# RWKV-7 attention with a merged mixture on one Trainium2 core: the state turned by whole transposes, and TensorE held to the order of the program text

## The chip, the cores and the metric

The kernel runs on one core of a Trainium2 chip. All data is in fp32. The metric is the device time of one execution in microseconds.

A core has five engines that run their own instruction queues and wait for one another by semaphores. TensorE does matrix products (the profile's PE, with its weight loads as PEld) and writes PSUM. VectorE (DVE), ScalarE (ACT) and GpSimd (POOL) do the elementwise work. SyncE (SP) issues most of the DMAs.

## What is computed

A recurrent attention block (4 batches, 8 heads, 768 tokens, head size 40) feeds a mixture of four experts (model width 320, hidden width 1024).

```python
def _attn_ref(r, k, v, w, a, b):
    for t in range(S):
        y[:, :, t] = np.einsum('bhd,bhde->bhe', rt, state)
        Sa = np.einsum('bhde,bhe->bhd', state, at)
        state_decay = state * wt[:, :, None, :] - np.einsum('bhd,bhe->bhde', Sa, bt)
        state = state_decay + np.einsum('bhd,bhe->bhde', vt, kt)

def _moe_ref(x, domain_probs, w1, w2):
    p = domain_probs / (domain_probs.sum(-1, keepdims=True) + 1e-09)
    for e in range(E):
        h = np.maximum(x @ w1[e], 0.0)
        out += p[:, e:e + 1] * (h @ w2[e])
```

## The kernel before

**Units.** The 768 tokens are cut into 12 chunks of 64, and the 4 batches into 2 pairs. One chunk of one pair is a unit: 24 units, numbered so that unit u is chunk u // 2 of pair u % 2. Inside a unit the recurrence is written as products of 64x64 blocks; from chunk to chunk only a state per batch and head is carried (`state`, one tile per batch, heads in four pairs j of two heads s). Unit u therefore needs the state that unit u - 2 has left.

**Stages of a unit.** `within` prepares what doesn't need the state: decays (`G`), transposes of the decay (`pg`) and of the scaled keys (`n_tok` to `NT` through `pNT`, `k_tok` to `KT` through `pKT`), score blocks (`pc`, `pf` in `F`, `pe` in `ET`, `pev` in `EV`). `substitute` inverts a triangular block of `F`: `blocks` are copied by VectorE and ScalarE, turned into `M` by VectorE, and a row-by-row elimination writes `Z`, from unit 2 on in some 60 small instructions of GpSimd (L559, L572). `merge` turns `Z` into `Qc` and `QTc` (VectorE, L583 and L585; both are kept in the order of the program text) and completes the inverse with the products `pY` and `pQ`. `step` brings in the state: `RH` (products of the state with `AT`), `psat` (copied to `SaT` and `SX`), `pxr` (two terms, one masked into `SX`, the other copied to `RS`), and `pdy`, from which VectorE makes the output `Y` and the new state. `Y` is brought to the layout of the mixture by products with `pick` (`pxT`, first two chunks) or by DMAs, as `xT`.

**The mixture.** Two units of a chunk go through the experts together. Its pieces wait in a list (`todo`): `up_last` and `up_main` (tile `ph`, lines 738 and 752, relu to `hs`), and `products` (tile `p`, line 873), seven half-size products in place of eight, with sums of weights and of `hs` made by VectorE (`a`). Each unit takes pieces from the list at four gaps. Units 0 and 1 use a plain form (`po`).

**The order.** The loop over u at the end calls the generators `w` (`within` of unit u + 2), `w_next`, `m` (`merge` of u + 1), `s` and `s_next` (`step` of u and u + 1), and the gaps in a written order; u < 5 is "early" and has an order of its own. A scheduler then places the instructions on each engine by its own estimates of when their inputs are ready. Only those wrapped in `tc.keep_in_program_order` keep the order of the text among themselves. On TensorE this concerns few before the change; on VectorE `Qc`, `QTc` and the first instructions of `substitute`, but not `Y`, the state updates, `n_tok` or `k_tok`.

**Quadrants.** Products of 64x64 blocks use a quarter of TensorE's array. `quadrants` issues them in an order in which four following ones use the four quarters: `row` is the half of the input partitions, `col` that of the output partitions. PSUM has five banks for tiles of tag `big` and three for `mm`, each in turn. In `step` the transposed state `SN`, needed by `pxr`'s second term, is made by 16 such products with an identity (`psn`, in the same two banks as `prh`; the profile shows both as `prn`).

Of the kernel before, what the change touches and what calls it, by code (L numbers as in the profile page):

```python
# [7 lines left out]
FP32 = mybir.dt.float32  # L8
# [7 lines left out]
def kernel(  # L16
# [53 lines left out]
    ps = ctx.enter_context(tc.tile_pool(name="ps", bufs=1, space=bass.MemoryType.PSUM))  # L70

# [121 lines left out]
    def load_raw(q, names):  # L193
# [3 lines left out]
        for x in names:  # L197
# [3 lines left out]
            for r in range(2):  # L201
                if x in "RV":

                    sets = ((slice(0, 8, 2), slice(r, 16, 4)), (slice(1, 8, 2), slice(3 - r, 16, 4)))
                else:
                    sets = ((slice(0, 8), slice(r, 16, 2)),)
# [99 lines left out]
    def normalize():  # L306
# [3 lines left out]
        for e in range(E):  # L310
            nc.tensor.transpose(out=pp[:, e * n:(e + 1) * n], in_=flat[:, :, e], identity=ident[0:n, 0:n])
# [24 lines left out]
    def turn(name, src, pinned=False):  # L336

        p = big(name)
        for j in range(NJ):
            ins = nc.tensor.transpose(out=p[:, j * P:(j + 1) * P], in_=src(j), identity=ident[:])  # L340
            if pinned and j == 0:
                tc.keep_in_program_order(ins)
# [14 lines left out]
    def d_half(j, s):  # L357
        return s ^ (j % 2)

    def of_d_half(x, r):  # L360

        return x.rearrange("p (jj four) e -> p jj four e", four=4)[:, :, slice(1, 3) if r else slice(0, 4, 3), :]

    BY_TOKENS = [(j, s, i) for j in range(NJ) for s, i in QUADS]
    BY_PAIRS = [(2 * j + x, s, i) for i in range(2) for j in range(2) for s, x in QUADS]
# [4 lines left out]
    def quadrants(p, lo, order, out_cols, *terms):  # L370


        for j, s, i in order:
            for n, term in enumerate(terms):
                row, col, at, lhsT, rhs = term(j, s, i)
                nc.tensor.matmul(  # L376
# [12 lines left out]
    def within(q):  # L389
# [31 lines left out]
        def turn_rv():  # L421
            VT = sb.tile([P, 2 * NJ, L], FP32, name="VT", tag="turned", bufs=3)
            q.RT = sb.tile([P, 2 * NJ, L], FP32, name="RT", tag="RT", bufs=2)
            for x, t in (("V", VT), ("R", q.RT)):
# [4 lines left out]
                to = t[:].rearrange("p (i j) t -> p j i t", i=2)  # L429
                nc.scalar.copy(out=to[:, 0::2], in_=p[:, 0::2])  # L430
                for r in range(2):
                    nc.scalar.copy(out=to[half(r), 1::2], in_=p[half(1 - r), 1::2])
# [145 lines left out]
    def merge(q):  # L578
# [16 lines left out]
        def two_heads(name, lhsT, rhs, to):  # L595
            p = big(name)
            for n in range(NJ):
                for r in range(2):
                    nc.tensor.matmul(  # L599
# [14 lines left out]

    def step(q, xT):
# [27 lines left out]
        psa = quadrants(p, 0, BY_TOKENS, L, lambda j, s, i: (  # L643
            i ^ s, d_half(j, s), j, RH[half(i ^ s), head(j, s), :], q.QT[half(i ^ s), head(j, s), :],
# [521 lines left out]
```

## Time and profile before

| | |
|---|---|
| Median of three runs | 1132.29 us (1129.44 to 1134.07) |
| The profiled execution | 1129.6 us |
| Its span, first to last instruction | 1127.5 us |
| Mean granted TensorE clock | 0.986 |
| TensorE busy in the whole span | 1083.1 us |
| TensorE's 16 `psn` products, one step (573.86 to 574.36) | 0.50 us |
| `pNT`'s four transposes (571.94 to 572.38) | 0.44 us |
| Chain that ended last: share of PE, of POOL | 67%, 10% |

A record of the profile gives an engine's instruction with its line, its operation, the tile that it writes, those that it reads, and its form. Several of one kind in a row are merged into one line with their number. Each quadrant product has two records. The time in square brackets is the engine's idle time before the instruction, with what ended it. Durations on TensorE overlap, so the time of a group there is read from its start to the start of the next.

### The profile page before, as it was taken

What the parts mean: (1) busy time and instruction counts of PE and PEld (TensorE: products, weight loads), DVE (VectorE), ACT (ScalarE), POOL (GpSimd) and SP (SyncE); (2) the same over time, 40 slices, a digit from 0 to 9 for tenths busy, and PEclk for the clock granted to TensorE, in tenths of its full rate; (3) what the DMA queues carried; (4) which work ended last, traced back from release to release, by engine and by line L of the source; (5) the groups of instructions that cost most, each with busy time, mean ns of one, the idle gap of its engine ahead of it and who ended that gap; (6) DMA issues with size and microseconds to landing.
All of it is one profiled execution on the core that took longest, in us unless ns stands there. A gap on an engine that the chain in (4) does not pass through costs nothing.

```text
span 1127.5 us, 38551 instructions
## 1 busy us (share of the span) xinstructions
PE 1083.1 (96%) x16100; PEld 963.2 (85%) x16100; DVE 758.8 (67%) x1553; ACT 353.0 (31%) x956; POOL 498.8 (44%) x1272
## 2 busy tenths in 40 slices
PE   6899997999999999999999999999999999999998
PEld 5777776788989889988989989989899999888887
DVE  8766547797766767677677677677677686553343
ACT  2323423332332332432432332332333323321110
POOL 5005727754625526437437347346346356340000
PEclk7899998999999999999999999999999999999999
DMA  7784553245253543644543543544553442231320
GB/s 118 214 239 125 130 113 71 71 108 126 77 130 88 122 102 99 141 103 93 143 104 88 143 103 90 142 96 96 133 114 86 122 110 63 76 90 57 108 90 12
DMA packets 268868, 122.18 MB, mean 108 GB/s; under 512 B 213736, under 2 KB 242072, under 8 KB 268696
## 3 DMA queue, kind: packets, MB, share of 16 engines
q1 hardware_dynamic: 265416, 119.12, 43.4%
q8 instruction: 127, 2.08, 0.8%
q10 hardware_dynamic: 3280, 0.61, 0.3%
q14 instruction: 45, 0.37, 0.1%
HBM read 111.79 MB, written 3.93 MB: 103 GB/s over the span
## 4 chain that ended last, share of the span: by engine, by line
PE 67%; POOL 10%; DVE 7%; issue 4%; ACT 2%; SPq 1%; DMA 1%; DVEq 0%; POOLq 0%
PE p L873 23%; PE ph L752 22%; PE ph L738 7%; POOL Z L572 6%; POOL Z L559 4%; PE pdy L376 2%; PE psat L376 2%; PE po L796 2%; DVE M L534 1%; PE pxr L376 1%; PE prn L376 1%; PE pQ L599 1%; PE pfe L376 1%; DVE G L406 1%; PE pc L376 1%
## 5 line engine op out<-in xcount | busy, mean ns | idle before, releaser
L752 PE MATMUL ph<-xT,w1p 128*128 128x256 f32 (+1 forms) x1520 | 342.7, 378 | 1.7 <-issue 1.7
L752 PEld LDWEIGHTS ph<-xT,w1p 128*128 128x128 f32 x1520 | 273.4, 190 | 63.1 <-issue 25.6
L572 POOL TENSOR_TENSOR Z<-Z 128x31 f32<-128x31 f32 (+7 forms) x704 | 257.2, 365 | 55.2
L867 DVE TENSOR_TENSOR a<-hs 128x512 f32<-128x512 f32 x220 | 153.8, 716 | 104.6 <-ACT hs L757 104.6
L559 POOL TENSOR_TENSOR Z<-M,Z 128x62 f32<-128x62 f32 (+7 forms) x352 | 144.0, 409 | 134.5 <-DVE M L550 108.7
L757 ACT ACTIVATE hs<-ph 128x512 f32<-128x512 f32 (+1 forms) x208 | 115.3, 564 | 235.3 <-PE ph L752 234.3
L873 PE MATMUL p<-sums,a 128*128 128x160 f32 x1056 | 165.1, 299 | 0.0
L873 PEld LDWEIGHTS p<-sums,a 128*128 128x128 f32 x1056 | 152.9, 190 | 2.3
L773 DVE SCALAR_TENSOR_TENSOR osb<-p,gate,osb 128x320 f32<-128x320 f32 (+1 forms) x243 | 107.9, 482 | 55.3 <-PE p L873 52.1
L531 POOL COPY below<-F 32x256 f32<-32x256 f32 x48 | 23.4, 488 | 219.5 <-ACT F L489 217.8
L738 PE MATMUL ph<-xT,w1p 64*64 64x256 f32 (+1 forms) x1520 | 111.1, 379 | 5.4 <-issue 5.4
L873 PE MATMUL p<-w,a 128*128 128x160 f32 x704 | 105.8, 301 | 0.9 <-ACT hs L757 0.5
L873 PE MATMUL p<-w,hs 128*128 128x160 f32 x704 | 102.9, 299 | 0.0
L873 PEld LDWEIGHTS p<-w,hs 128*128 128x128 f32 x704 | 100.3, 190 | 2.2
L873 PEld LDWEIGHTS p<-w,a 128*128 128x128 f32 x704 | 98.3, 190 | 3.6 <-ACT hs L757 3.6
L591 POOL COPY QT<-QTc 32x256 f32<-32x256 f32 x96 | 49.3, 513 | 91.4 <-DVE QTc L585 44.9
L738 PEld LDWEIGHTS ph<-xT,w1p 64*64 64x64 f32 x1520 | 66.1, 135 | 14.3 <-issue 9.8
L534 DVE STREAM_TRANSPOSE M<-blocks 128x1024 f32<-128x1024 f32 x24 | 47.2, 1968 | 33.9 <-ACT blocks L528 33.7
L679 ACT COPY RS<-pxr 64x256 f32<-64x256 f32 x88 | 32.2, 366 | 115.0 <-DVE SX L387 73.6
L419 DVE RECIPROCAL gp<-gp 128x320 f32<-128x320 f32 x24 | 51.7, 2153 | 0.8
L516 ACT COPY EV<-pev 64x160 f32<-64x160 f32 x96 | 23.4, 286 | 88.1 <-PE pev L376 87.7
L583 DVE STREAM_TRANSPOSE Qc<-Z 128x256 f32<-128x256 f32 x24 | 15.1, 631 | 49.1 <-POOL Z L572 48.9
(151 smaller groups left out, 1427.9 us busy)
## 6 DMA issues: line engine op xcount, KB each, us to landing
w1p<-in_moe_w_dram SPq DMA_DIRECT2D x95, 512.0 KB
w1p<-in_moe_w_dram SPq DMA_DIRECT2D x190, 64.0 KB
w<-in_moe_w_dram SPq DMA_DIRECT2D x4, 1280.0 KB
sums<-in_moe_w_dram SPq DMA_DIRECT2D x9, 512.0 KB
natW<-in_w_dram SPq DMA_DIRECT2D x48, 80.0 KB
natB<-in_b_dram SPq DMA_DIRECT2D x48, 80.0 KB
natK<-in_k_dram SPq DMA_DIRECT2D x48, 80.0 KB
out_dram<-osb SPq DMA_DIRECT2D x46, 80.0 KB
```

Of the source, the lines that this page charges most:

```text
L376: nc.tensor.matmul(out=p[row][half(col), lo + at * out_cols:lo + (at + 1) * out_cols], lhsT=lhsT, rhs=rhs, start=(n == 0), stop=(n == len( ...
L419: pin(nc.vector.reciprocal(out=gp[:], in_=gp[:]))
L534: ins = nc.vector.transpose(out=M[:], in_=cols)
L559: ins = eng.tensor_tensor(out=Z[:, 1:3, 0:n, j + 1:Q], in0=M[:, j:j + 2, None, j + 1:Q].to_broadcast([P, 2, n, m]), in1=Z[:, here, 0:n, j: ...
L572: eng.tensor_tensor(out=z[:, 0], in0=z[:, 0], in1=z[:, x], op=ALU.add)
L591: ins = nc.gpsimd.tensor_copy(out=q.QT[quarter(i), :, quarter(i % 2)], in_=QTc[quarter(i)])
L738: nc.tensor.matmul(out=ph[i][half(c), f, :], lhsT=w1.last[part(i), f, half(c)], rhs=xT[part(i), 2, :], start=(f == 0), stop=False,)
L752: nc.tensor.matmul(out=ph[i][:, f, :], lhsT=w1.main[:, g, at * P:(at + 1) * P], rhs=xT[:, g, :], start=False, stop=(g == 1 and f == HF // ...
L757: nc.scalar.activation(out=h[:, i * HF // 2:(i + 1) * HF // 2, 0:n], in_=ph[i][:], func=ACTF.Relu,)
L773: nc.vector.scalar_tensor_tensor(out=to, in0=p, scalar=sc, in1=to, op0=ALU.mult, op1=ALU.add)
L867: nc.vector.tensor_tensor(out=t[:], in0=x, in1=y, op=op)
L873: nc.tensor.matmul(out=p[:, n * HD:(n + 1) * HD], lhsT=a[:, f, :], rhs=b[:, f, :], start=(f == 0), stop=(f == HF - 1),)
```

## The change

Four things are done.

- `matmul` and `transpose` wrap every TensorE instruction in `keep_in_program_order`.
- The 16 `psn` products of `step` go. A new function `turn_state` makes four full 128x128 transposes of the state into a bank of their own and one copy to `SN`, which has its own buffer. The loop calls it for unit u + 1 after the decay's transposes (`pg`) of unit u + 2. Tiles of tag `step` get two buffers in place of three.
- Which head lies in which half of `VT`, `RT`, `SaT`, `SX` and `RS` is set by j % 2 in place of s ^ (j % 2). The orders of the quadrants, the DMAs of the raw inputs and the copies of `VT` and `RT` (four of 64 partitions each, where there were one of 128 and two of 64) and of `RS` (two in place of four) follow from this.
- In the loop for u >= 5, `merge`'s first product and the first part of the next `step` (`prh`) come before `pc`, and `merge`'s second product comes after the first part of an up piece (`lead`), before its main part.

The order in which TensorE's instructions stand in the compiled kernels, one unit of the steady part, by tile and number of products:

```
before: pNT 4  pKT 4  pc 16  prn 32  pY 8  ph 16  p 16  pQ 8  pfe 16  ph 8  psat 32  ph 8  p 12  pe 16  pxr 32  ph 16  p 16  pg 4  pev 16  pdy 32  ph 16  p 12
after:  pNT 4  pKT 4  pY 8  prh 16  pc 16  ph 8  pQ 8  ph 8  p 16  pfe 16  ph 8  psat 32  ph 8  p 12  pe 16  pxr 32  ph 16  p 16  pg 4  psn 4  pev 16  pdy 32  ph 16  p 12
```

and VectorE's, around the merge of unit 14:

```
before: RT  Y 2  state  Y  state 2  n_tok  state  k_tok  Qc  G  QTc  G
after:  RT  Qc  Y 2  state  Y  state 2  n_tok  state  k_tok  QTc  G 2
```

The diff, without the places where only the name of the call changes:

```diff
@@ -69,6 +69,12 @@
     sb = ctx.enter_context(tc.tile_pool(name="sb", bufs=1))
     ps = ctx.enter_context(tc.tile_pool(name="ps", bufs=1, space=bass.MemoryType.PSUM))
 
+    def matmul(**k):
+        return tc.keep_in_program_order(nc.tensor.matmul(**k))
+
+    def transpose(**k):
+        return tc.keep_in_program_order(nc.tensor.transpose(**k))
+
     def big(name):
         return ps.tile([P, 512], FP32, name=name, tag="big", bufs=5)
 
@@ -201,7 +207,7 @@
             for r in range(2):
                 if x in "RV":
 
-                    sets = ((slice(0, 8, 2), slice(r, 16, 4)), (slice(1, 8, 2), slice(3 - r, 16, 4)))
+                    sets = [(slice(y, 8, 2), slice(2 * r + y, 16, 4)) for y in range(2)]
                 else:
                     sets = ((slice(0, 8), slice(r, 16, 2)),)
                 for n, hs in sets:
...
@@ -354,15 +360,17 @@
     def head(j, s):
         return 2 * j + s
 
-    def d_half(j, s):
-        return s ^ (j % 2)
+    def of_d(x, j, s, i, n=64):
+        return x[64 * (j % 2):64 * (j % 2) + n, 4 * i + 2 * (j // 2) + s, :]
 
     def of_d_half(x, r):
 
-        return x.rearrange("p (jj four) e -> p jj four e", four=4)[:, :, slice(1, 3) if r else slice(0, 4, 3), :]
+        return x.rearrange("p (jj four) e -> p jj four e", four=4)[:, :, 2 * r:2 * r + 2, :]
 
     BY_TOKENS = [(j, s, i) for j in range(NJ) for s, i in QUADS]
-    BY_PAIRS = [(2 * j + x, s, i) for i in range(2) for j in range(2) for s, x in QUADS]
+    BY_D_TOKENS = [(2 * jj + r, s, i) for jj in range(2) for s in range(2) for r, i in QUADS]
+    BY_TOKENS_D = [(2 * jj + x, s, r ^ s) for jj in range(2) for s in range(2) for r, x in QUADS]
+    BY_D_HEADS = [(2 * jj + r, s, i) for jj in range(2) for i in range(2) for r, s in QUADS]
 
     def banks(name):
         return [big(f"{name}{x}") for x in range(2)]
...
@@ -426,10 +434,10 @@
                     turn_raw(t[:], n["raw" + x][:])
                     continue
                 p = turn(f"p{x}T", tok(n["padded" + x]), q.u == 1)[:].rearrange("p (j i t) -> p j i t", i=2, t=L)
-                to = t[:].rearrange("p (i j) t -> p j i t", i=2)
-                nc.scalar.copy(out=to[:, 0::2], in_=p[:, 0::2])
+                to = t[:].rearrange("p (i jj s) t -> p s jj i t", i=2, s=2)
                 for r in range(2):
-                    nc.scalar.copy(out=to[half(r), 1::2], in_=p[half(1 - r), 1::2])
+                    for y in range(2):
+                        nc.scalar.copy(out=to[half(r), y], in_=p[half(y), r::2])
             return VT
 
         if q.u == 1:
@@ -445,8 +453,8 @@
             return n["paddedV"][:, :, 0:D] if q.u < PADDED else n["V"][:]
 
         def causal_scores(VT):
-            pc = quadrants(banks("pc"), 0, BY_TOKENS, L, lambda j, s, i: (
-                d_half(j, s), i, j, of_slots(VT, d_half(j, s), j, i, D), of_slots(q.RT, d_half(j, s), j, i, D),
+            pc = quadrants(banks("pc"), 0, BY_D_TOKENS, L, lambda j, s, i: (
+                j % 2, i, 2 * (j // 2) + s, of_d(VT, j, s, i, D), of_d(q.RT, j, s, i, D),
             ))
             for r in range(2):
                 pin(causal(of_d_half(q.VC[:, :, D:D + L], r), pc[r]), q.start)
...
@@ -612,6 +620,19 @@
         two_heads("pQ", Qc, Y, q.QT[:, :, quarter(1)])
         yield
 
+    def turn_state(q):
+
+        if q.start:
+            return
+        psn = big("psn")
+        for i in range(2):
+            for jj in range(2):
+                x = state[q.b[i]][:, 2 * jj:2 * jj + 2, :].rearrange("p j d -> p (j d)")
+                at = (2 * i + jj) * P
+                transpose(out=psn[:, at:at + P], in_=x, identity=ident[:])
+        q.SN = sb.tile([P, 2, 2, 2, 64], FP32, name="SN", tag="SN", bufs=1)
+        nc.scalar.copy(out=q.SN[:].rearrange("p i jj s e -> p (i jj s e)"), in_=psn[:])
+
     def step(q, xT):
 
         st = [state[bb] for bb in q.b]
@@ -620,28 +641,20 @@
         if q.start:
             RH = q.EV
         else:
-            p = banks("prn")
-            prh = quadrants(p, 0, BY_TOKENS, D, lambda j, s, i: (
+            prh = quadrants(banks("prh"), 0, BY_TOKENS, D, lambda j, s, i: (
                 s, i ^ s, j, of_slots(q.AT, s, j, i), st[i][half(s), j, 0:D],
-            ))
-
-            psn = quadrants(p, NJ * D, BY_PAIRS, 64, lambda j, s, i: (
-                s, d_half(j, s), 2 * i + j // 2, st[i][half(s), j, :], ident[half(s), half(s)],
             ))
             RH = RHs()
             for s in range(2):
                 nc.vector.tensor_tensor(
                     out=of_slot(RH[:], s)[:, :, 0:D], in0=prh[s], in1=of_slot(q.EV[:], s)[:, :, 0:D], op=ALU.add,
                 )
-            SN = sb.tile([P, 2, 2 * 2, 64], FP32, name="SN", tag="step", bufs=3)
-            for s in range(2):
-                nc.scalar.copy(out=SN[:, s], in_=psn[s])
         yield
 
 
         p = banks("psat")
-        psa = quadrants(p, 0, BY_TOKENS, L, lambda j, s, i: (
-            i ^ s, d_half(j, s), j, RH[half(i ^ s), head(j, s), :], q.QT[half(i ^ s), head(j, s), :],
+        psa = quadrants(p, 0, BY_TOKENS_D, L, lambda j, s, i: (
+            i ^ s, j % 2, 2 * (j // 2) + s, RH[half(i ^ s), head(j, s), :], q.QT[half(i ^ s), head(j, s), :],
         ))
         SX = SXs()
         if not q.end:
@@ -649,7 +662,7 @@
             pst = quadrants(*at, BY_TOKENS, D, lambda j, s, i: (
                 i ^ s, i, j, q.QT[half(i ^ s), head(j, s), :], RH[half(i ^ s), head(j, s), 0:D],
             ))
-        SaT = sb.tile([P, NJ, 2, L], FP32, name="SaT", tag="step", bufs=3)
+        SaT = sb.tile([P, NJ, 2, L], FP32, name="SaT", tag="step", bufs=2)
         for x in range(2):
             nc.scalar.copy(out=SaT[:, :, x, :], in_=psa[x])
         if not q.end:
@@ -660,25 +673,21 @@
         yield
 
         p = banks("pxr")
-        px = quadrants(p, 0, BY_TOKENS, L, lambda j, s, i: (
-            d_half(j, s), i, j, SaT[half(d_half(j, s)), j, i ^ s, :], of_slots(q.RT, d_half(j, s), j, i),
+        px = quadrants(p, 0, BY_D_TOKENS, L, lambda j, s, i: (
+            j % 2, i, 2 * (j // 2) + s, SaT[half(j % 2), 2 * (j // 2) + s, i ^ s, :], of_d(q.RT, j, s, i),
         ))
         if not q.start:
-            prs = quadrants(p, NJ * L, BY_PAIRS, L, lambda j, s, i: (
-                d_half(j, s), s, 2 * (j // 2) + i, SN[half(d_half(j, s)), s, 2 * i + j // 2, :],
-                of_slots(q.RT, d_half(j, s), j, i),
+            prs = quadrants(p, NJ * L, BY_D_HEADS, L, lambda j, s, i: (
+                j % 2, s, 2 * (j // 2) + i, q.SN[half(j % 2), i, j // 2, s, :], of_d(q.RT, j, s, i),
             ))
         for x in range(2):
             ins = causal(of_d_half(SX[:, :, D:D + L], x), px[x])
             if q.u == 0:
                 tc.keep_in_program_order(ins)
         if not q.start:
-            RS = sb.tile([P, NJ, 2, L], FP32, name="RS", tag="step", bufs=3)
+            RS = sb.tile([P, NJ, 2, L], FP32, name="RS", tag="step", bufs=2)
             for x in range(2):
-                for s in range(2):
-                    nc.scalar.copy(
-                        out=RS[half(s), x ^ s::2], in_=prs[x][half(s)].rearrange("p (j i) t -> p j i t", i=2),
-                    )
+                nc.scalar.copy(out=RS[:, x::2], in_=prs[x].rearrange("p (jj i) t -> p jj i t", i=2))
         yield
 
 
@@ -688,7 +697,7 @@
             lambda j, s, i: (i, s, j, q.K[half(i), head(j, s), :], q.VC[half(i), head(j, s), lo:D + L]),
             lambda j, s, i: (i, s, j, q.N[half(i), head(j, s), :], SX[half(i), head(j, s), lo:D + L]),
         )
-        Y = sb.tile([P, NJ, 2, L], FP32, name="Y", tag="step", bufs=3)
+        Y = sb.tile([P, NJ, 2, L], FP32, name="Y", tag="step", bufs=2)
         Gv = q.G.rearrange("p (j i) t -> p j i t", i=2)
         for i in range(2):
             nc.vector.tensor_tensor(
...
@@ -1077,6 +1086,8 @@
         if early:
             run(s, 1)
         run(w, 1)
+        if u + 1 < NU:
+            turn_state(units[u + 1])
         if not early:
             run(w_next)
         run(s)
@@ -1094,7 +1105,11 @@
             go(load_raw(begin(u + 3), "WA"))
             load(units[u + 3], "WBKV")
             later.extend(load_raw(units[u + 3], "VR"))
-        run(w, 2)
+        run(w, 1)
+        if not early:
+            run(m, 1)
+            run(s_next, 1)
+        run(w, 1)
 
         soon = u in (2, 3, 4)
         if soon:
@@ -1102,14 +1117,12 @@
         if early:
             run(m, 1)
         else:
-            run(s_next, 1)
+            lead()
             run(m, 1)
         if soon:
             substitute(units[u + 2], nc.gpsimd)
         gap(2)
 
-        if not early:
-            run(m, 1)
         if not soon:
             run(w, 1)
         if not early:
```

More of the change, by code (lines that the diff above doesn't have):

```diff
@@ L310, in normalize @@
         for e in range(E):
-            nc.tensor.transpose(out=pp[:, e * n:(e + 1) * n], in_=flat[:, :, e], identity=ident[0:n, 0:n])
+            transpose(out=pp[:, e * n:(e + 1) * n], in_=flat[:, :, e], identity=ident[0:n, 0:n])
         nc.scalar.copy(out=gate[:], in_=pp[:, 0:E * n].rearrange("p (e b c) -> p c b e", b=B // 2, c=NC))
@@ L339, in turn @@
         for j in range(NJ):
-            ins = nc.tensor.transpose(out=p[:, j * P:(j + 1) * P], in_=src(j), identity=ident[:])
+            ins = transpose(out=p[:, j * P:(j + 1) * P], in_=src(j), identity=ident[:])
             if pinned and j == 0:
@@ L375, in quadrants @@
                 row, col, at, lhsT, rhs = term(j, s, i)
-                nc.tensor.matmul(
+                matmul(
                     out=p[row][half(col), lo + at * out_cols:lo + (at + 1) * out_cols], lhsT=lhsT, rhs=rhs,
@@ L598, in two_heads @@
                 for r in range(2):
-                    nc.tensor.matmul(
+                    matmul(
                         out=p[half(r), n * 2 * Q:(n + 1) * 2 * Q], lhsT=lhsT[half(r), 2 * n:2 * n + 2, :],
@@ L710, in step @@
             for n, (g, j) in enumerate(PLACES):
-                nc.tensor.matmul(
+                matmul(
                     out=px[:, g * P:(g + 1) * P], lhsT=pick[:, n, :], rhs=Y[:, j].rearrange("p i t -> p (i t)"),
@@ L737, in up_last @@
                 for i in range(2):
-                    nc.tensor.matmul(
+                    matmul(
                         out=ph[i][half(c), f, :], lhsT=w1.last[part(i), f, half(c)],
@@ L751, in up_main @@
                     at = i * HF // 2 + f
-                    nc.tensor.matmul(
+                    matmul(
                         out=ph[i][:, f, :], lhsT=w1.main[:, g, at * P:(at + 1) * P],
@@ L795, in down @@
             for f in range(NF):
-                nc.tensor.matmul(
+                matmul(
                     out=po[:], lhsT=hs[e][f // HF][:, f % HF, 0:P], rhs=w2_sb[e][:, f, :],
@@ L872, in products @@
                 for f in range(HF):
-                    nc.tensor.matmul(
+                    matmul(
                         out=p[:, n * HD:(n + 1) * HD], lhsT=a[:, f, :], rhs=b[:, f, :],
@@ L971, in keep_warm @@
         for _ in range(n):
-            ins = nc.tensor.matmul(out=warm[:, 0:P], lhsT=ident[:], rhs=ident[:], start=True, stop=True)
+            ins = matmul(out=warm[:, 0:P], lhsT=ident[:], rhs=ident[:], start=True, stop=True)
             tc.keep_in_program_order(ins)
```

## The prediction

> **What bounds the kernel now.** I read the page first, then busy time by stretch, then the timeline of one late unit engine by engine, then the order in which the compiled instructions of both versions stand on each engine.
>
> The page's engine rows (busy us, share of the span, instructions):
>
> ```profile
> PE 1083.1 (96%) x16100; PEld 963.2 (85%) x16100; DVE 758.8 (67%) x1553; ACT 353.0 (31%) x956; POOL 498.8 (44%) x1272
> ```
>
> Busy time by stretch, of which the fourth is ten units of the steady part (us, then each engine's busy us and instructions):
>
> ```profile
> 486.00:915.00 429.00, 428.31 (x6685) 388.39 (x6684) 310.97 (x630) 144.00 (x390) 217.87 (x552) 1.00 0.46 110
> ```
>
> TensorE is busy 428.3 of 429.0 us there: the steady part is TensorE's work and nothing else, 42.87 us a unit. Its idle time is all earlier. What matters for the change is how close the other engines run behind it. The timeline of TensorE where the transposes of unit 15 and the merge of unit 14 meet:
>
> ```profile
> 614.80 0.60 PE L340 MATMUL pNT<-ident,n_tok 128*128 128x128 f32 x4
> 615.24 0.60 PE L340 MATMUL pKT<-ident,k_tok 128*128 128x128 f32 x4
> 615.77 0.69 PE L376 MATMUL pc<-RT,VT 40*64 40x64 f32 x32
> 616.29 0.63 PE L376 MATMUL prn<-state,AT 64*64 64x40 f32 x32
> 616.73 0.67 PE L376 MATMUL prn<-ident,state 64*64 64x64 f32 x32
> 617.22 0.57 PE L599 MATMUL pY<-QTc,below 64*64 64x64 f32 x14
> ```
>
> and VectorE and GpSimd at the same place:
>
> ```profile
> 609.12 0.72 DVE L694 TENSOR_TENSOR Y<-pdy,RS 128x256 f32<-128x256 f32 x2
> ...
> 609.99 0.80 DVE L699 TENSOR_TENSOR Y<-Y,G 128x512 f32<-128x512 f32 x1
> ...
> 611.36 0.48 DVE L455 SCALAR_TENSOR_TENSOR n_tok<-natB,gp 128x320 f32<-128x320 f32 x1
> ...
> 612.09 0.65 DVE L459 TENSOR_TENSOR k_tok<-natK,gp 128x320 f32<-128x320 f32 x1
> 615.13 0.64 DVE L583 STREAM_TRANSPOSE Qc<-Z 128x256 f32<-128x256 f32 x1 [2.39 <-POOL Z L572]
> ...
> 615.94 0.40 DVE L585 STREAM_TRANSPOSE QTc<-Qc 128x256 f32<-128x256 f32 x1
> ```
> ```profile
> 614.58 0.52 POOL L572 TENSOR_TENSOR Z<-Z 128x8 f32<-128x8 f32 x2
> ```
>
> The reader should see three distances. n_tok is ready at 611.84, 2.96 us before pNT takes it. QTc is ready at 616.34, 0.88 us before pY takes it. And VectorE stands idle 2.39 us at Qc because GpSimd finishes Z only at 615.1; everything behind Qc on VectorE would have waited too, but before it stood all that TensorE needed next.
>
> [...] while VectorE waits the 2.39 us for Z, nothing of its own runs. [...] Here a gap of 3.42 us before pY at 193.39 left the next 13 records at 0.59 us, the same as elsewhere, while one of 5.97 us at 20.91 made pev's 32 records take 1.32 us against 0.68. [...] here four 128x128 transposes take 0.44 us before more of their kind (pNT) and 0.53 us before quadrant products (pKT), so a switch is about 0.09 us.
>
> **The change part by part.**
> 1. *The state turned by transposes.* It removes 16 quadrant products a step (616.73 to 617.22: 0.49 us) in 22 steps, and adds four 128x128 transposes right behind pg's four, in the same mode: 0.44 us by pNT's row. Net -0.05 us a step, -1.1 us in all, if TensorE is the bound. The state it reads was updated a whole unit earlier, so it waits for nothing. On ScalarE two SN copies of 0.372 us become one of about 0.59 (NT's row, same shape), and RS goes from four copies of 0.366 to two of about 0.37. ScalarE is busy 144 of 429 us in the steady part; worth nothing.
> 2. *New orders of the quadrants* (pc, psat, pxr, prs). psat's first term takes about 0.55 us, pxr's 0.47 with as many products; between 0 and -0.08 us a unit. I take -0.04, so -1.
> 3. *One more PSUM tile and the 'step' tag with two buffers.* Tile by tile the releases come as early as before; pc's second bank waits for the KT copy, which ends 1.71 us after pNT starts, and pc comes at 1.83. Nothing, at most 0.2 us a unit.
> 4. *pY and the state's product move ahead of pc, pQ ahead of the main part of up.* In the steady part pY now follows pKT at once, 0.97 us after pNT's start, where it stood at 2.42. QTc is ready at 1.54. So pY waits, unless QTc comes earlier. That is a loop: from psat's start over SaT, SX, blocks, M, GpSimd's 21 us of Z and Qc to QTc's end is 30.5 us (mean of nine units, 30.3 to 30.7), plus 0.15 us to pY (118.59 to 118.73 in unit 2). From pY back to psat TensorE took 11.58; with the state's product (0.44) and pc (0.49) now inside, 12.5. Sum 43.15, against 42.87 before: +0.3 us a unit. Before, the same loop had 42.2 and hid.
> 5. *VectorE's order, which nobody states.* Fixing TensorE's order makes the scheduler place the rest anew. The compiled order of the changed kernel has, in eight of the units (merge of units 8, 10, ... 22), VectorE's Qc ahead of both Y additions, the state updates, n_tok and k_tok, and QTc behind them. The order before has k_tok first, then Qc, in all of these. Qc waits for Z. So n_tok, which had 2.96 us to spare, now comes after Z. From Qc's start: Qc 0.5, then the stretch 609.12 to 611.84 (2.72) to n_tok's end, to 612.74 (3.62) for k_tok's, QTc 0.4. With 0.15 for the signal, pNT can start at 3.35 us after Qc's start, pKT at 4.25, pY at 4.8.
>
> Pairs of units: the good one takes 43.15 by the loop of step 4. The bad one takes 12.5 (pY to psat) + 29.27 (psat to Qc, 30.5 less 1.23) + 4.8 = 46.6. Sum 89.7, against 2 x 42.87 = 85.7: +4.0 a pair, eight pairs, +32. TensorE waits in both, so part 1's saving is eaten there. What could lower it: GpSimd is alone at the end of Z when VectorE stands still. That is worth 0 to 1 us a pair; I take 0.1 to 0.2, so +31, between +24 and +34. The gap before pNT is about 3.4 us, [...] I take no loss of clock.
>
> 6. *The first five units with TensorE in the stated order.* Before, the scheduler filled waits with pieces of the mixture:
>
> ```profile
> 52.05 0.62 PE L738 MATMUL ph<-xT,w1p 64*64 64x128 f32 x16
> ...
> 57.79 0.31 PE L376 MATMUL pev<-VC,ET 64*64 64x40 f32 x2 [0.43 <-DVE ET L387]
> ...
> 59.82 4.47 PE L796 MATMUL po<-w,hs 128*128 128x320 f32 x16
> ```
>
> Now pev stands before all of ph. ET is ready near 58.1, so some 5 us of ph run after it and not before: +4 at 59.82. Of this 1.96 us come back where ph waited for osb at 68.83; then pQ (Yq's copies, about 1.3 us after pY), pc (VT and RT, eight copies of 64 partitions where there were six, +0.7) and pev of unit 1 (0.93 seen, about 2 us of ph no longer ahead of it) wait uncovered, +1 to +3. F of unit 2 and with it GpSimd's chain move by the same 4 us, so the wait for QTc at 118.73 (0.26) doesn't take it back. In units 2 to 4 the pxT products lose their fillers (about 1 us each, two times), while pdy's wait for SX at 207.72 (1.47) goes, as ph now stands ahead. Sum +4, bounds +1 and +9. Load waits by DMA move with the rest.
>
> Sum against the profiled run of 1129.6 us (span 1127.5): -1 + 31 + 4 + about 1 for the first steady units = +35, so 1165. The median of the runs is 2.7 us above that profiled run.
>
> **The rivals.**
> - *Faster (6%).* Z is done before VectorE comes to Qc, so the new order holds up nothing and TensorE stays the bound. Place: Qc in the eight units. It decides from Z ending about 6 us earlier (609.1, where Y started) and QTc within 0.97 us of pNT. Price: 22 x 0.05 and 24 x 0.08 off, and 2 us of early waits: -5, so 1125. For it: TensorE's steady part has no idle time, so less work counts in full. Against it: Z ended at 615.1 in this unit and its 21 us of GpSimd aren't touched; F moves by 0.5 us only.
> - *Held up only a little (12%).* Z ends some 3 us earlier, within n_tok's reserve, or VectorE's chain behind Qc is much quicker without GpSimd: then only the loop of step 4 (17 units x 0.3) and the early part: +9, so 1139.
> - *The clock falls too (4%).* [...] about 2.5 us more in each of eight units: +20, so 1185.
> - The forecast: 78%, its own range 1155 to 1177.
>
> **How the numbers follow.** 0.5% is 5.7 us, about what can be told from no change. The forecast, the third rival and nearly all of the second are slower: 0.78 + 0.04 + 0.09 = 0.91. Same: 0.03 of the second and 0.01 of the first, 0.04. Faster 0.05. The range takes the forecast's range and reaches down to the middle of the second rival's way: 1143 to 1178.
>
> **What would show it.** Right: a wait of TensorE at pNT for VectorE's n_tok, 3 to 4 us in each of eight units, every second one; VectorE idle about 5 us at Qc for GpSimd's Z there; pY waiting about 0.4 us for QTc in the others; units of 43.1 and 46.6 us by turns; TensorE busy near 93%. Step 1: psn's four transposes in 0.44 us. Step 6: pev waiting some 5 us near 53. Wrong: pNT without waits in the steady part, or an even 42.8 us a unit.

## The result and the profile after

The changed kernel takes 1160.03 us (median of six runs, 1158.21 to 1164.2) against 1133.24 us (1129.44 to 1135.38) for the kernel before on the same chip: a ratio of 1.024, 95% interval 1.022 to 1.027. The profiled execution took 1160.9 us and its span 1158.8, 31.3 us more than before. The forecast was 1165 us, range 1143 to 1178.

The engine row of the page for TensorE, and the chain that ended last by engine (the other lines of both views are left out):

```profile
PE 1088.7 (94%) x15484; PEld 969.4 (84%) x15484; DVE 756.3 (65%) x1553; ACT 338.9 (29%) x896; POOL 493.3 (43%) x1272
...
PE 57%; POOL 15%; DVE 8%; issue 5%; ACT 4%; DMA 2%; SPq 1%; POOLq 0%; DVEq 0%
```

TensorE has fewer instructions than before and is busy a little longer. The chain tells the rest: it ran through TensorE for 67% of the span and through GpSimd for 10%; now these are 57% and 15%. TensorE waits, and its mean granted clock falls from 0.986 to 0.976. Where, the busy time by stretch shows: of the kernel before (first fence) and after (second), the columns being the stretch, its length, then busy us and instructions of PE, PEld, DVE, ACT and POOL, the granted clock, the DMA share and GB/s.

```profile
0.00:145.00 145.00, 122.11 (x1874) 102.56 (x1875) 97.15 (x225) 48.15 (x140) 57.97 (x168) 0.93 0.67 163
145.00:263.00 118.00, 106.82 (x1789) 88.53 (x1788) 85.84 (x162) 40.70 (x115) 69.26 (x162) 0.96 0.41 91
263.00:409.00 146.00, 142.51 (x2203) 129.41 (x2202) 103.72 (x210) 47.63 (x128) 68.64 (x173) 1.00 0.45 107
409.00:943.00 534.00, 531.71 (x8325) 481.65 (x8324) 386.70 (x782) 180.19 (x489) 267.95 (x680) 1.00 0.47 111
```
```profile
0.00:145.00 145.00, 114.67 (x1814) 97.22 (x1815) 91.73 (x215) 49.05 (x142) 52.69 (x153) 0.89 0.65 156
145.00:263.00 118.00, 110.85 (x1767) 93.93 (x1765) 93.27 (x176) 40.25 (x109) 76.89 (x183) 0.97 0.43 99
263.00:409.00 146.00, 135.71 (x1922) 121.98 (x1921) 95.48 (x192) 41.26 (x108) 64.08 (x164) 0.95 0.42 101
409.00:943.00 534.00, 520.05 (x7681) 471.06 (x7680) 371.50 (x756) 163.31 (x432) 256.60 (x660) 1.00 0.45 107
```

A reader should compare TensorE's idle time, the length less the busy time. It goes from 22.9 to 30.3 us in the first stretch, falls from 11.2 to 7.2 in the second, and rises from 3.5 to 10.3 and from 2.3 to 14.0 in the third and fourth. The starts of `pNT` in the two traces give the lateness: after is 7.4 us late near 144 us, 3.6 us early at 263, 10.2 late at 409, 28.3 late at 943 and 31.3 late at the end. In the third stretch it grows by 13.8 us, the idle time by 6.8 only. The rest is busy time, at a granted clock of 0.95 where the kernel before had 1.00.

The place where the transposes meet the merge, in the timelines after: VectorE, TensorE and GpSimd.

```profile
623.79 0.65 DVE L234 STREAM_TRANSPOSE RT<-rawR 128x512 f32<-128x512 f32 x1
628.32 0.63 DVE L591 STREAM_TRANSPOSE Qc<-Z 128x256 f32<-128x256 f32 x1 [3.88 <-POOL Z L580]
628.81 0.73 DVE L703 TENSOR_TENSOR Y<-pdy,RS 128x256 f32<-128x256 f32 x2
...
630.74 0.49 DVE L463 SCALAR_TENSOR_TENSOR n_tok<-natB,gp 128x320 f32<-128x320 f32 x1
...
631.37 0.49 DVE L467 TENSOR_TENSOR k_tok<-natK,gp 128x320 f32<-128x320 f32 x1
631.77 0.45 DVE L593 STREAM_TRANSPOSE QTc<-Qc 128x256 f32<-128x256 f32 x1
```
```profile
631.29 0.66 PE L76 MATMUL pNT<-ident,n_tok 128*128 128x128 f32 x4 [1.89 <-DVE n_tok L463]
632.02 0.63 PE L76 MATMUL pKT<-ident,k_tok 128*128 128x128 f32 x4
632.57 0.70 PE L73 MATMUL pY<-QTc,below 64*64 64x64 f32 x13
```
```profile
627.78 0.51 POOL L580 TENSOR_TENSOR Z<-Z 128x8 f32<-128x8 f32 x2
```

This is the hold that the prediction named. GpSimd ends `Z` at 628.29, `Qc` starts at once, and everything that stands behind it on VectorE comes after it: `n_tok` ends at 631.23, and TensorE, idle 1.89 us, takes it at 631.29. Before, `n_tok` had been ready 2.96 us ahead of need. Behind this wait the clock falls too, 1.7 us after `pNT` starts:

```profile
633.00:636.00 3.00, 3.00 (x86) 2.87 (x84) 2.82 (x8) 1.29 (x5) 1.82 (x3) 0.50 0.08 19
```

From `pNT` to `pQ` TensorE takes 5.20 us here, and 3.60 us behind the wait of 1.75 us at 721.13, where the clock stays. The same happens behind the hold at 358.88, and behind none of the other six. The waits of TensorE over the whole span (us in total, times, longest) have `pNT` on top, eight times at the holds and twice in the first units:

```profile
PE pNT L76 <- DVE n_tok L463: 15.5, 10, 1.9
PE pev L73 <- DVE ET L395: 12.7, 3, 6.0
PE ph L73 <- issue: 8.5, 3, 3.5
PE pQ L73 <- ACT Yq L614: 4.8, 11, 1.8
```

One sentence of the text ahead of the prediction has to be made exact: it says that pinned instructions keep the order of the text among themselves. The compiled orders fit a narrower reading, that `Qc`'s pin holds it only behind the VectorE instruction traced just before it, the turn of `RT`. In both orders `Qc` stands somewhere behind `RT`, in the changed one directly behind it and ahead of `n_tok` and `k_tok`, though the text has these first.

### The profile page after: what moved, and what is told of

It is laid out like the page before. It is cut to its first block, busy times and chain, and to the rows that moved or that the text cites. A ratio compares the mean times of both kernels' runs of the same rounds, so it can differ in the third digit from the quotient of the medians.

```text
span 1158.8 us, 37184 instructions
## 1 busy us (share of the span) xinstructions
PE 1088.7 (94%) x15484; PEld 969.4 (84%) x15484; DVE 756.3 (65%) x1553; ACT 338.9 (29%) x896; POOL 493.3 (43%) x1272
## 4 chain that ended last, share of the span: by engine, by line
PE 57%; POOL 15%; DVE 8%; issue 5%; ACT 4%; DMA 2%; SPq 1%; POOLq 0%; DVEq 0%
PE ph L73 25%; PE p L73 17%; POOL Z L580 10%; POOL Z L567 6%; DVE M L542 2%; PE psat L73 2%; PE po L73 2%; PE pdy L73 2%; PE pY L73 1%; PE pfe L73 1%; PE pc L73 1%; ACT SX L672 1%; PE pxr L73 1%; DMA w1p<-in_moe_w_dram 1%; PE pQ L73 1%
## 5 line engine op out<-in xcount | busy, mean ns | idle before, releaser
L73 PE MATMUL ph<-xT,w1p 128*128 128x256 f32 (+3 forms) x3040 | 454.2, 382 | 12.1 <-issue 8.5
L73 PEld LDWEIGHTS ph<-xT,w1p 64*64 64x64 f32 (+1 forms) x3040 | 341.3, 165 | 79.2 <-issue 33.8
L580 POOL TENSOR_TENSOR Z<-Z 128x31 f32<-128x31 f32 (+7 forms) x704 | 249.8, 355 | 55.2
L567 POOL TENSOR_TENSOR Z<-M,Z 128x62 f32<-128x62 f32 (+7 forms) x352 | 147.1, 418 | 156.3 <-DVE M L558 130.4
L599 POOL COPY QT<-QTc 32x256 f32<-32x256 f32 x96 | 50.2, 523 | 105.2 <-DVE QTc L593 75.4
L690 ACT COPY RS<-pxr 128x256 f32<-128x256 f32 x44 | 15.4, 372 | 137.7 <-DVE SX L395 74.6
L234 DVE STREAM_TRANSPOSE VT<-rawV 128x512 f32<-128x512 f32 x21 | 14.9, 711 | 42.4 <-DMA rawR<-in_r_dram 23.9
L73 PE MATMUL pdy<-VC,k_tok 64*64 64x104 f32 (+1 forms) x768 | 41.7, 258 | 0.0
L73 PE MATMUL pdy<-SX,n_tok 64*64 64x104 f32 (+1 forms) x768 | 40.8, 246 | 0.4 <-DVE SX L395 0.4
```

The costliest lines, as they stand in the source:

```text
L73: return tc.keep_in_program_order(nc.tensor.matmul(**k))
L567: ins = eng.tensor_tensor(out=Z[:, 1:3, 0:n, j + 1:Q], in0=M[:, j:j + 2, None, j + 1:Q].to_broadcast([P, 2, n, m]), in1=Z[:, here, 0:n, j: ...
L580: eng.tensor_tensor(out=z[:, 0], in0=z[:, 0], in1=z[:, x], op=ALU.add)
L599: ins = nc.gpsimd.tensor_copy(out=q.QT[quarter(i), :, quarter(i % 2)], in_=QTc[quarter(i)])
L690: nc.scalar.copy(out=RS[:, x::2], in_=prs[x].rearrange("p (jj i) t -> p jj i t", i=2))
```

## The experiments

Theories at the start: **H**, VectorE's hold at `Qc` is the loss; **T**, TensorE waits because it is kept in the stated order; **C**, TensorE's clock falls behind the new waits. The times of the first four kernels are set against 1133.5 us for the kernel before on their chip, those of the last three against 1130.81.

**e1: `Qc` behind `k_tok`, and nothing else.** TensorE's compiled order is that of the changed kernel.

```diff
-        pin(nc.vector.tensor_tensor(out=q.K[:, :, 0:D], in0=n["K"][:], in1=gp[:], op=ALU.mult))
+        ins = nc.vector.tensor_tensor(out=q.K[:, :, 0:D], in0=n["K"][:], in1=gp[:], op=ALU.mult)
+        pin(ins)
+        k_ins[0] = ins.ins
...
-        tc.keep_in_program_order(nc.vector.transpose(out=dealt(Qc[:]), in_=q.Z))
+        if EARLY < q.u < NU - 1:
+            with tc.issue_after(k_ins[0]):
+                nc.vector.transpose(out=dealt(Qc[:]), in_=q.Z)
+        else:
+            tc.keep_in_program_order(nc.vector.transpose(out=dealt(Qc[:]), in_=q.Z))
```

> The changed kernel with VectorE's Qc queued behind k_tok (units 6 to 22); TensorE's order is the changed kernel's, instruction by instruction. Theory H (the hold: Qc waits for GpSimd's Z ahead of n_tok and k_tok in eight units, about 3.3 us each): pNT waits for n_tok no more after 300 us, 1160 falls by 8 x 3.3 = 26 to about 1134. Rival T (TensorE's stated order itself costs the time, by the loop from psat over Z and QTc to the earlier pY and by waits that nothing fills): stays at 1150 or above. Rival C (the lower granted clock, 0.976): no change.

Measured: 1130.62 us (1126.17 to 1133.41), ratio to the kernel before 0.997 [0.995, 0.999], span 1124.0. By the medians one place in VectorE's queue is worth 29 us, where 26 were expected. Between the two profiled executions it is 34.8 us of span, but e1's is the fastest of its thirteen, and 3.3 of the 34.8 stand there at 263 us already, ahead of the first hold. The stretch of the steady part that the prediction showed, and the same transposes in TensorE's timeline, in e1:

```profile
486.00:915.00 429.00, 427.00 (x6399) 390.56 (x6395) 311.43 (x631) 135.50 (x359) 217.09 (x551) 1.00 0.46 109
```
```profile
612.09 0.60 PE L76 MATMUL pNT<-ident,n_tok 128*128 128x128 f32 x4
612.53 0.60 PE L76 MATMUL pKT<-ident,k_tok 128*128 128x128 f32 x4
613.06 0.62 PE L73 MATMUL pY<-QTc,below 64*64 64x64 f32 x13
```

`pNT` has no bracket: it does not wait, with TensorE pinned as in the changed kernel. H holds. The mean granted clock is 0.985 again, so the falls that C speaks of follow the waits and are no loss beside H.

**e2: the changed kernel without the pins on TensorE.**

```diff
     def matmul(**k):
-        return tc.keep_in_program_order(nc.tensor.matmul(**k))
+        return nc.tensor.matmul(**k)
     def transpose(**k):
-        return tc.keep_in_program_order(nc.tensor.transpose(**k))
+        return nc.tensor.transpose(**k)
```

> The changed kernel without the pins on TensorE's instructions, all else as in the change; the compiled order has Qc ahead of n_tok in seven units (from unit 10 on) and a filled early part as in the kernel before. Theory H: seven times 3.3, about 1153, with pNT waiting for n_tok in these seven. Rival T: the pins are the cost, so it comes back to about 1133.

Measured: 1161.58 us (1159.29 to 1162.31), ratio 1.024 [1.021, 1.027]. Its compiled order has `Qc` ahead of `Y` in seven units, from 10 on, and its list of TensorE's waits begins so:

```profile
PE pNT L76 <- DVE n_tok L463: 15.8, 9, 2.3
```

The scheduler is free to put other products first, and TensorE waits at `pNT` as long as in the pinned kernel (15.8 us, nine times, against 15.5, ten times). T falls: the loss is there without the pins. What the prediction called the scheduler placing VectorE anew does not need them; without them it makes the same hold, and which other part of the change leads to it was not tested. The time is 8.6 us above the 1153 expected. VectorE stands 7.82 us at `AT` for a late DMA here, near 461 us, `ph` waits 3.75 us, and the unit takes 50.2 us. So what the pins cost or save by themselves is not shown by this run.

**e3: the kernel before with the hold put in.** In eight units the merge is traced ahead of the step and what VectorE does up to `k_tok` is issued behind `Qc`; TensorE's order is that of the kernel before.

```diff
+        held = u >= 7 and u % 2 == 1 and u + 1 < NU
+        if held:
+            run(m, 1)
+            behind.append(tc.issue_after(qc_ins[0]))
+            behind[0].__enter__()
         run(s)
...
-        if not early:
+        if not early and not held:
             run(m, 1)
```

> The kernel before with VectorE's Qc put ahead of Y, the state updates, n_tok and k_tok in eight units (merge of 8, 10, ... 22) and nothing else; TensorE's order is that of the kernel before. Theory H: eight times about 3.3 to 4, so 1133 becomes 1158 to 1164, with pNT waiting for n_tok. Rival T and rival C: no change beyond 3 us, since TensorE's order and pY's place are the old ones.

Measured: 1178.26 us (1175.54 to 1182.7), ratio 1.039 [1.036, 1.043]. The hold makes the kernel before slower without the rest of the change, and by more than in the changed kernel: 92.11 us a pair of units against 85.77, and 14 us above the upper end of what was expected. Two timelines of e3, VectorE and TensorE:

```profile
630.46 0.62 DVE L587 STREAM_TRANSPOSE Qc<-Z 128x256 f32<-128x256 f32 x1 [5.83 <-POOL Z L576]
630.93 0.67 DVE L230 STREAM_TRANSPOSE RT<-rawR 128x512 f32<-128x512 f32 x1
631.53 0.40 DVE L589 STREAM_TRANSPOSE QTc<-Qc 128x256 f32<-128x256 f32 x1
631.85 0.71 DVE L698 TENSOR_TENSOR Y<-pdy,RS 128x256 f32<-128x256 f32 x2
```
```profile
634.65 1.09 PE L342 MATMUL pNT<-ident,n_tok 128*128 128x128 f32 x4 [3.68 <-DVE n_tok L457]
635.53 1.06 PE L342 MATMUL pKT<-ident,k_tok 128*128 128x128 f32 x4
636.52 1.14 PE L378 MATMUL pc<-RT,VT 40*64 40x64 f32 x32
```

The turn of `RT` and `QTc` stand ahead of `Y` here, which makes `n_tok` another 0.92 us late (630.93 to 631.85). And TensorE's wait of 3.68 us is followed by records of nearly twice their length: from `pNT`'s start to `pY`'s it takes 4.48 us (634.65 to 639.13), where the kernel before took 2.42 (614.80 to 617.22). The wait and this make 5.7 of some 6.3 us a pair. So the loss that C names exists: from 486 to 915 us e3's granted clock is 0.97, where the kernel before and the changed one have 1.00. In the changed kernel the clock falls behind two of the eight holds.

**e1b: e1 with the turn of the raw decays into `G` pinned in its place in the text, for every unit from 8 on.** In e1 VectorE still stands at this turn while its DMA is late, near 270 us, and `ph` waits 6.3 us in three places, 3.7 at the longest.

```diff
-            pin(turn_raw(ahead[:, i], n["rawW"][:, NJ * i:NJ * i + NJ, :]))
+            pin(turn_raw(ahead[:, i], n["rawW"][:, NJ * i:NJ * i + NJ, :]), q.u > EARLY + 2)
```

> As before it, and G's turn of the raw decays also kept behind the elimination's first instructions on VectorE, so that its wait for a DMA stands no longer ahead of the additions that free PSUM for the next up piece. Theory H says nothing on it. Theory D (the waits of the up piece's lead near 279, 327 and 377 us, 8.5 us together, come from VectorE standing at a transpose whose DMA is late): about 5 us less than the run with Qc alone, near 1129. Rival: those waits are for the weights' own DMA, then they stay and so does the time.

Measured: 1137.35 us, ratio 1.003 [1.002, 1.004]: slower than e1. This wait goes (1.0 us of `ph`'s is left), but the steady units take 43.96 us against e1's 42.93, as `Z` takes 1.2 us longer. GpSimd in e1 (first fence) and e1b (second), then VectorE in e1b, at the same place of the elimination:

```profile
591.10 0.57 POOL L584 TENSOR_TENSOR Z<-Z 128x29 f32<-128x29 f32 x2
```
```profile
593.53 1.92 POOL L584 TENSOR_TENSOR Z<-Z 128x29 f32<-128x29 f32 x2
```
```profile
593.29 1.24 DVE L416 TENSOR_TENSOR_SCAN G<-G,first 128x512 f32<-128x512 f32 x1
```

The two instructions take 1.92 us in place of 0.57 when `G`'s scan runs beside them: the pin had moved the scan from behind `QTc` to the start of the next `Z`. So the pin is right for the units whose load is late, and wrong for the rest.

**e5: e1 with `pc`, `prh`, `pY` and `pQ` in their old places.**

```diff
-        run(w, 1)
-        if not early:
-            run(m, 1)
-            run(s_next, 1)
-        run(w, 1)
+        run(w, 2)
+        if not early:
+            run(s_next, 1)
+            run(m, 1)
...
-        else:
-            lead()
-            run(m, 1)
...
         gap(2)
+        if not early:
+            run(m, 1)
```

> The changed kernel with Qc behind k_tok, and with pc, the state's product and pY of the steady part in the places that they have in the kernel before (pQ after the up piece). Theory L (with Qc mended, the steady part runs at the loop psat - M - Z - QTc - pY - psat, 12.25 + 29.3 + 1.2 + 0.15 = 42.9 us, not at TensorE's own work): the loop shrinks to about 42.3, pY has slack again, TensorE's work of about 42.75 us sets the pace: 0.15 to 0.2 us less in each of 16 units, 2.5 to 3 us less than with Qc alone, so about 1128. Rival P (TensorE's own work sets it there too): the same 1130.6.

Measured: 1126.63 us, ratio 0.996 [0.994, 0.997]. By the whole time this can't be told from e1, as the intervals of the two ratios overlap. The traces tell it: TensorE is busy 428.78 of the 429 us of the steady stretch (e1: 427.00), and a unit takes 42.74 us against 42.93. Moving `pY` forward had closed the loop that step 4 of the prediction computed; moving it back opens it again, and TensorE is the bound.

**e6: e5 with `G`'s turn pinned in units 8 to 10 only.** The diff is e1b's with `8 <= q.u <= 10` as its condition.

> As the run before it, and G's turn kept behind the elimination's first instructions for units 8, 9 and 10 alone, where its DMA is late. Theory D (VectorE standing at G's turn holds the additions that free PSUM for the up piece's lead): the waits of TensorE near 275 to 325 us, 3.7 us at the longest, go; 4 to 6 us less, about 1123. Rival: the weights' DMA is what is late, then nothing changes.

Measured: 1117.7 us, ratio 0.988 [0.984, 0.993], 8.9 us less than e5 by the medians and 7.4 us of span. In the traces 4.3 us of the 7.4 arise in the three units with late loads, from the `pY` near 265 us to the one near 395 (e5 133.88, e6 129.55). 3.0 us stand there before, where VectorE and TensorE have the same order in both kernels, and are not put down to the pin. So the late loads that the pin mends cost some 4 us in e5. VectorE in the changed kernel (first fence) and TensorE's timeline there (second):

```profile
273.22 0.93 DVE L234 STREAM_TRANSPOSE G<-rawW 128x256 f32<-128x256 f32 x2 [4.76 <-DMA rawW<-in_w_dram]
...
278.55 0.37 DVE L782 SCALAR_TENSOR_TENSOR osb<-p,minus_gate,osb 128x160 f32<-128x160 f32 x1
...
372.68 0.71 DVE L234 STREAM_TRANSPOSE AT<-rawA 128x512 f32<-128x512 f32 x1 [7.51 <-DMA rawA<-in_a_dram]
```
```profile
279.02 1.55 PE L73 MATMUL ph<-xT,w1p 64*64 64x256 f32 x11 [3.22 <-issue]
...
377.19 1.55 PE L73 MATMUL ph<-xT,w1p 64*64 64x256 f32 x11 [3.50 <-issue]
```

and VectorE in e6 at the first of these places:

```profile
268.87 1.29 DVE L884 TENSOR_TENSOR a<-hs 128x512 f32<-128x512 f32 x2 [2.63 <-ACT hs L774]
...
271.48 0.38 DVE L790 SCALAR_TENSOR_TENSOR osb<-p,minus_gate,osb 128x160 f32<-128x160 f32 x1
```

In the changed kernel VectorE stands 4.76 and 7.51 us at inputs that have not landed, and the additions into `osb`, which empty PSUM for the next piece `ph`, stand behind. "issue" in the bracket says that the profile names no releaser; that it is the PSUM that `osb` frees was read from the order of the two, and from `ph`'s waits after 250 us being gone in e6, where `osb` no longer stands behind the load.

The kernel before has such waits too, with shorter ones of TensorE behind them (1.18, 2.31 and 1.38 us); VectorE and TensorE at one of them:

```profile
362.95 0.93 DVE L228 STREAM_TRANSPOSE G<-rawW 128x256 f32<-128x256 f32 x2 [4.88 <-DMA rawW<-in_w_dram]
```
```profile
369.15 0.87 PE L738 MATMUL ph<-xT,w1p 64*64 64x256 f32 x11 [2.31 <-issue]
```

So the pin of `G` might help the kernel before as well. That was not tried.

**e7: e6 with TensorE pinned only from the loop's u = 2 on.** The wrappers pin where `stated[0]` is set, and the loop sets it to `u >= 2`.

> As the run before it, and TensorE's pins only from unit 2 on, so that the first two units are filled by the scheduler. Theory F (in the stated order pev and pQ of units 0 and 1 wait uncovered, about 5 us more than before by 150 us): 3 to 5 us less, about 1119. Rival (GpSimd's chain for units 2 to 5 takes the time back): within 1 us of the run before it.

Measured: 1113.52 us (1109.06 to 1114.44), ratio 0.983 [0.977, 0.989], the lowest median of all, though its interval overlaps e6's. Its engine row of the page and its steady stretch:

```profile
PE 1076.4 (97%) x15484; PEld 962.8 (87%) x15484; DVE 762.0 (69%) x1553; ACT 338.2 (30%) x896; POOL 500.5 (45%) x1272
```
```profile
486.00:915.00 429.00, 429.00 (x6487) 391.29 (x6480) 313.72 (x632) 137.66 (x366) 216.87 (x550) 1.00 0.45 111
```

TensorE is never idle in the steady part, and a unit takes 42.73 us against 42.89 before. The change, with VectorE's order, the place of `pY`, the turn of `G` and the start put right, is 1.7% faster than the kernel before. Of the 15.2 us of span between the two, 9.7 are won by the `pY` near 260 us, 1.3 in the next three units and 3.0 in the twelve after these. As the turn of `G` might have helped the kernel before too, the 1.7% is not shown to be the worth of the change alone.

## Why the prediction was right, and where it was not

The parts of a unit, from the starts of these groups in the traces, means over units 12 to 21 in us (held: the unit in which `Qc` stands ahead in after and e3; free: the other):

| | pY to psat | psat to Qc | Qc to QTc's end | to pY | unit |
|---|---|---|---|---|---|
| before, both | 11.57 | 29.30 | 1.20 | 0.82 | 42.89 |
| after, free | 13.11 | 29.79 | 1.21 | 0.15 | 44.25 |
| after, held | 12.25 | 28.39 | 3.89 | 0.35 | 44.89 |
| e1, both | 12.25 | 29.29 | 1.20 | 0.19 | 42.93 |
| e3, held | 11.64 | 28.52 | 1.46 | 7.21 | 48.84 |
| e5, both | 11.29 | 29.19 | 1.20 | 1.06 | 42.74 |

- **Step 5, the hold: right, and it decides.** Predicted +4.0 us a pair, measured 89.14 - 85.77 = 3.4 against before; e1, which leaves everything else of the change in place, gives 89.14 - 85.86 = 3.3. Eight pairs would make 26, where the forecast had 31. The reason given for the new order, that TensorE's order is fixed, is wrong: e2 has the hold without it. The compiled order itself had been read rightly. The held unit was put at 12.5 + 29.27 + 4.8 and measures 12.25 + 28.39 + 4.24. The largest miss is the middle term: it is 0.9 us shorter than in the kernel before (0.8 in e3), which fits GpSimd running alone while VectorE stands (in the kernel before, a record of `Z` of one form took 344 to 348 ns alone and 672 to 807 beside `a`); the prediction took 0.1 to 0.2 for that, out of a bound of 1. The free unit measures 44.25 and not 43.15, with 13.11 us from `pY` to `psat`: in one of five the clock had fallen (13.92), in another `ph` waits 1.26 us (13.71), and the other three average 12.6. So the wait at `pNT` is 1.2 to 1.9 us and not 3.4, and the units do not differ by 3.5 us, though their sum nearly does as forecast.
- **Step 4, the loop: right.** 43.15 us predicted for the loop with nothing held, 42.93 in e1, where `pY` starts 0.15 to 0.23 us behind `QTc`; undone in e5.
- **Step 1: right.** In the trace of after, `pg` and `psn` take 0.97 us a step together, from start to start, where before took 1.02; -0.05 was predicted. With step 2 it is seen only where TensorE is the bound, as -0.16 us a unit in e7, where -0.09 was predicted for the two.
- **Step 6, the first five units: the wrong sign.** `pev` waits as foretold:

```profile
52.69 0.65 PE L73 MATMUL pfe<-AT,KT 64*64 64x64 f32 x32
58.96 1.22 PE L73 MATMUL pev<-VC,ET 64*64 64x40 f32 x29 [5.62 <-DVE ET L395]
```

  and the kernel is 7.4 us late at 144 us. But the prediction let only 1.47 us come back in units 3 to 5, and 11.0 come back by 263 us, in which both kernels issue the same products but for those of `psn`. 4.7 us are waits: TensorE's idle time between the two marks falls from 11.2 to 6.5 us, as 5.5 us of `pY` for `QTc` and 1.7 us of `pdy` for `SX` are gone and 2.2 us of `pxT` are 0.7. The other 6.3 us are busy time (110.84 us before, 104.51 after). The clock is part of that: between the marks it stood at half for 10.2 us before and for 6.8 after, and 91 records against 23 last over 1.5 times the median of their form. Half of the difference is 1.7 us; the rest was not followed. The sum was -3.6 at 263 and not +4.
- **"Load waits by DMA move with the rest": wrong.** Three units from 263 to 409 us lose 13.8 us: 6.8 of idle time and 7.0 of busy time, with the clock at half for 13.7 us in all, where the kernel before had none. One hold is a part of it. e1, with no hold, still loses 5.4 us there. That leaves VectorE at `G` and `AT` for late DMAs (4.76, 5.09 and 7.51 us): it had waited for them before as well, but `ph` now waits 3.22, 1.73 and 3.50 us behind.

So the sum was right partly because its terms erred against each other: forecast +31 and +4, measured by the marks -3.6 to 263 us, +13.8 to 409 with one hold, and +21.1 behind with seven, +31.3 in all. At 3.3 us a hold the eight make 26.4 and leave 8.5 for the late loads; at the 3.0 us that the last seven show they leave 10.8. That the late loads, which the sum did not have, made up for the better start and the smaller holds is luck.

- **The rivals.** Z ending early, or the hold being small, is refuted by the 3.88 us of VectorE in front of `Qc` and by e1. The fall of the clock, put at 4%, came true in part. Its price of 2.5 us a unit was the author's estimate, which no trace gave: behind the hold at 631.29 the fall added 1.60 us (5.20 less 3.60, from `pNT` to `pQ`), in e3 2.06 (4.48 less 2.42, from `pNT` to `pY`). The prediction took no loss of clock, and leaned on the gap of 3.42 us at 193.39 in the kernel before: its 13 records of `pY` are fast (0.59 us), but from 194.3 us on the granted clock is 0.50, as the last section shows. In the changed kernel the clock falls behind two of the eight holds, and at the load waits of 3.22 and 3.50 us (11 `ph` records in 1.55 us, against 0.87 in e1's steady part). Over the span, 0.024 of 1158.8 us against 0.014 of 1127.5 are up to 12 us of clock within the 31.3; up to, because some of that time TensorE stood idle: at 278 us the clock was at half for 1.0 us before the wait of 3.22 us ended.

## What to carry to other kernels

When a change moves instructions that a scheduler places, read the compiled order of every engine before the run: here `Qc`, which waited 3.88 us for GpSimd, held up all that stood behind it on VectorE, `n_tok` and `k_tok` too, which don't need it. Hold such an instruction behind the work that others wait for, as e1 does with one line, and pin a load's first use behind what empties PSUM only where that load is late (in three units it won some 4 us, e6 against e5; in all from 8 on it lost 6.7, e1b against e1). Then test the rest of the change by itself: with four such places put right the kernel here was 1.7% faster than the one before, and 2.4% slower without. Give a mend that fits the kernel before, as the turn of `G`, to that one too, or the gain can't be divided between the two.

## What was not expected of the hardware

- **GpSimd beside VectorE.** The same two `Z` instructions took 0.57 us in e1 and 1.92 us in e1b beside `G`'s scan. In the kernel before, over 300 to 950 us, records of one form of `Z` (128x76) took 344 to 348 ns with VectorE idle (8 of them) and 672 to 807 ns beside the additions `a` (19); three more, which an `a` met for 0.2 us or less, took 344 to 348. Another form, 128x54, took in the changed kernel 299 to 307 ns alone (7), 304 to 308 beside the reciprocal into `gp` (18), and 672 beside `Y<-Y,G` where that met it for 0.5 us (2). The reciprocal has one input; the scan, `a` and this `Y` have two. That the number decides is not shown beyond these forms. The prediction had priced it at 0.1 to 0.2 us a pair.
- **Waits and the clock.** In these traces a single wait's length doesn't say when TensorE slows. Waits of 3.22, 3.50 and 3.68 us were followed by records of nearly double length (1.55 us against 0.87 for 11 of `ph`, 1.09 against 0.60 for four of `pNT`), and so was the one of 3.42 us in the kernel before, 0.9 us after its end. Its first records came before the fall, which is what the prediction saw:

```profile
194.30:197.70 3.40, 3.40 (x78) 2.94 (x70) 3.37 (x5) 1.86 (x8) 2.30 (x5) 0.50 0.81 223
```

  But shorter ones did it too. In the kernel before, 1.47 us for `SX` stood among others, and the granted clock (third column from the end) halved behind them:

```profile
206.00:208.00 2.00, 0.53 (x7) 0.20 (x5) 2.00 (x5) 0.30 (x1) 1.73 (x4) 0.99 0.30 54
208.00:210.00 2.00, 2.00 (x37) 1.68 (x36) 1.97 (x3) 1.17 (x4) 1.72 (x4) 0.50 0.07 12
210.00:212.00 2.00, 2.00 (x47) 1.95 (x41) 1.62 (x2) 0.43 (x1) 1.66 (x5) 0.66 0.00 0
```

  TensorE worked 0.53 of 2 us and then ran 3.4 us at half speed. In the changed kernel 1.65 us at `pNT` and 1.03 us at `pc`, ending 2.3 us apart, left `pc` at 1.14 us against 0.69 in the kernel before's steady part. Of the eight lone waits of 1.2 to 1.9 us at the holds, those of 1.76 (358.88) and 1.89 us (631.29) were followed by half speed within 1.7 us, others of 1.75, 1.76 and 1.78 us were not. Where a fall begins varies: 0.9 us behind the end of the wait of 3.42 us, 1.7 us behind that of 1.89, and 1.0 us ahead of the end of that of 3.22. What decides it is not shown. The longest single wait was 1.47 us ahead of the fall in the view above, and 1.89 ahead of the one at 631.29. A wait priced at its own length was too cheap: 1.89 us at 631.29 came with 1.60 us more from `pNT` to `pQ`.
